# A two-branch attention kernel on one core: TensorE's order inside the recurrence written out by hand, and its weight loads moved from one DMA queue to another

## The chip, the core and the metric

The kernel runs on one core of a Trainium2 chip. The metric is device time in microseconds (us) of one execution. Engines are named as the profile names them: PE is TensorE (PEld its weight loads), DVE is VectorE, ACT is ScalarE, POOL is GpSimd and SP is SyncE; SPq, ACTq and POOLq are the queues through which these engines issue DMAs. "Granted clock" is the share of TensorE's full clock that it was given.

## What is computed

Two attention branches read the same x (2048 tokens of 576 features), and a sigmoid gate mixes their results row by row:

```python
x = A_x
g = _sigmoid((x * gate_w).sum(-1, keepdims=True))
a = _A_ref(x, A_mem0, A_Wq, A_Wk, A_Wv, A_Wo, A_seg_len)
b = _B_ref(x, B_wqkv, B_wo)
return g * a + (1 - g) * b
```

Branch A is a recurrence over 64 segments of 32 tokens. Each segment prepends 8 memory rows, projects the 40 rows to q, k and v with 32 heads of 128, applies masked softmax attention, projects back to 576 features with Wo, and hands its first 8 output rows on as the memory of the next segment:

```python
h = jnp.concatenate([mem, xs], axis=1)
...
o = jnp.einsum('bhte,hed->btd', o, Wo)
mem = o[:, :M, :].copy()
```

Branch B is plain softmax attention over all 2048 tokens with 32 heads of 18. It has no recurrence.

## The kernel before

**Stages.** A prologue (lines 318 to 467) transposes x, projects branch B's q, k and v into DRAM scratch (`qtd`, `ktd`, `vgd`), computes the gate and loads branch A's weights `wv`, `wq`, `wk` in 18 pieces, each one DMA (12 of 1 MB, 6 of 256 KB). `last_tokens` (line 287) then projects, for a batch of 16 segments, the last 8 tokens of each segment, which don't depend on the memory: 24 steps of 20 or 5 matmuls for the first batch before the recurrence, and 72 for the other three, which are fillers inside it. Then comes the recurrence (line 607), and at the end branch B's output projection with the gate (lines 750 to 812).

**Branch B as units.** Branch B's attention is a generator of 512 units, `b_steps`. A unit takes 512 queries and 128 keys of four heads: four score matmuls `sb` (line 208) into one PSUM tile of four banks, of which there is one buffer, two exponentials `etb` on ACT (line 229), and the four value matmuls `ob` (line 190) of the unit before. After 16 units the sums are turned and divided on DVE (lines 241 to 253, "the divide" below) and stored. `b_advance(1)` issues one unit; the kernel calls it between pieces of the prologue, inside the recurrence and in the end part.

**One segment of the recurrence.** `project` (line 631) multiplies the 32 rows `ht` with a quarter-packed weight block into PSUM (`pvv`), DVE copies it to `tm`; two such for each of q, k, v. `turn` transposes q and k (`pt`, line 647; DVE copies to `qt`, `kt`, line 652). The scores `psh` (line 677) go through an exponential on ACT (`et`, line 685) and a minimum on DVE that applies the mask (line 687). A matmul with a block of ones gives the sums `pss` (line 700), whose logarithm `lt` and the exponential of its negative `rq` (ACT, lines 702 and 704) give the reciprocal; DVE multiplies it in (line 705). The weighted values `pso` (line 713) are copied to `ot` (line 721), `out_project` multiplies with `wo` into `acc` (line 555) in two column spans, `split` takes each span apart into a high and a low half `hl` on DVE (lines 566 and 567), and `fold` (line 576) sums the packed quarters and transposes in one matmul (`pw3`); three copies put the first rows into the next `ht` (lines 738 to 740). Every fourth segment leaves a group of 32 last-token rows whose projection `finish_group` does one segment later. `fill` runs one step of `last_tokens`, or, when these are used up, four matmuls `idle` (line 485) whose result nobody reads. All these PSUM tiles share one tag `pb` with three buffers.

**What sets the order.** Nothing but a few manual edges is fixed by hand: a list scheduler orders each engine's instructions by its priorities and modelled readiness, within the data dependences. `tick()` spreads branch B's units over 16 places of a segment:

```python
per_tick = (total_steps - done[0] - NKB * 3 // 4) / n_seg / 16
```

The DMAs of one queue are issued in its order. The prologue's stores of projected q, k, v go through SP, and after every second store `store` places one piece of the weights behind it:

```python
d = nc.sync.dma_start(out=out, in_=in_)
stores[0] += 1
if stores[0] % 2 == 0:
    w = next(wgen, None)
```

POOL's queue carries the transposed x, the zero rows of `qtd` and `ktd` (`zt`) and the loads of branch B's `qch`, `kch` and `vch`.

Of the kernel before, what the change touches and what calls it, by code (L numbers as in the profile page):

```python
# [16 lines left out]
def kernel(  # L17
# [118 lines left out]
    def load_weights(w, src):  # L136
        w2 = src.rearrange("d h e -> d (h e)")
        for c in range(NF):
            yield nc.sync.dma_start(out=w[0][:, c, :], in_=w2[c * P:(c + 1) * P, :])
        for two in range(2):  # L140
            yield nc.sync.dma_start(
# [21 lines left out]
    def b_steps():  # L163
        kch, vch, qch = {}, {}, {}

# [15 lines left out]
        for gq in range(GB * NQC):  # L181
# [21 lines left out]
            for kb in range(NKB):  # L203
# [29 lines left out]
                before = ets  # L233
                yield
# [3 lines left out]
            HC = QC // 2  # L238
            for hf in range(2):
                tq = bint.tile([P, HC // 32, 32], FP32, name="tq")  # L240
                nc.vector.transpose(
                    out=tq[:, :, :].rearrange("p b e -> p (b e)"), in_=ob[:, hf * HC:(hf + 1) * HC]
                )
                rtb = bint.tile([P, HC // 32, 1], FP32, name="rtb")
# [10 lines left out]
                )  # L255
            if gq == GB * NQC - 1:
                last_stage.append(stage)
            else:
                for j in range(4):
                    f = (4 * g + j) * DhB  # L260
                    nc.sync.dma_start(
                        out=otd[f:f + DhB, qc * QC:(qc + 1) * QC], in_=stage[32 * j:32 * j + DhB, :]
                    )
# [58 lines left out]
    with ExitStack() as pctx:  # L322
# [16 lines left out]
        for n in range(NT):  # L339
# [22 lines left out]
            if (n + 1) * sn % SG == 0:  # L362
                q = (n + 1) * sn // SG - 1
                nc.gpsimd.dma_start(
# [3 lines left out]
        def all_weights():  # L368
            for w, src in ((wv, A_Wv), (wq, A_Wq), (wk, A_Wk)):
                yield from load_weights(w, src)  # L370

        wgen = all_weights()
        stores = [0]

        def store(out, in_):

            d = nc.sync.dma_start(out=out, in_=in_)
            stores[0] += 1
            if stores[0] % 2 == 0:
                w = next(wgen, None)  # L380
                if w is not None:
                    issue_behind(w, d)
# [10 lines left out]
        def project_qk(blk, share):  # L393
            stg = pw.tile([P, S], BF16, name="stg")
            for t in range(NQC):
# [10 lines left out]
                if share != 2 and t % 2 == 1:  # L406
                    b_advance(1)
            f = blk * P
            while f < (blk + 1) * P:
# [3 lines left out]
                store(out=(qtd, ktd)[which][h // 4, r:r + n, :], in_=stg[f - blk * P:f - blk * P + n, :])  # L413
# [10 lines left out]
        def project_vb(hf, ticks):  # L424
            for kb in range(NKB):
# [12 lines left out]
                store(  # L438
# [3 lines left out]
                if ticks != 2 and kb % 4 == 3:  # L442
                    b_advance(1)
# [26 lines left out]
    for i, _ in enumerate(last_tokens(0, 4)):  # L470
        b_advance(i % 2)
# [7 lines left out]
    def fill():  # L479
        if next(later, "end") == "end":  # L480
# [55 lines left out]
    pace = [0.0]  # L536
# [43 lines left out]

    pending = []

    def finish_group():

        if not pending:
            return
# [260 lines left out]
```

## Time and profile before

| what | value |
|---|---|
| median of 2 runs | 1947.96 us (1944.79 to 1951.13) |
| the profiled execution's own time | 1947.82 us |
| its span, first to last instruction | 1946.1 us |
| mean granted clock | 0.953 |
| busy, share of span | PE 88%, ACT 60%, DVE 49%, PEld 45%, POOL 9% |
| chain that ended last | PE 62%, ACT 16%, DVE 11%, DMA 6% |

A row of a group reads: line, engine, operation, output<-inputs, shapes, count, then total busy us and mean ns of one, then the idle time of the engine just before these instructions and who ended it. A row of the timeline reads: start, duration, engine, line, operation, count, and in brackets the idle time before it with its releaser. Matmuls are pipelined, so that a group of them is shorter than the sum of its durations, and a busy PE isn't PE at its peak.

### The profile page before, as it was taken

What the parts mean: (1) busy time and instruction counts of PE and PEld (TensorE: products, weight loads), DVE (VectorE), ACT (ScalarE), POOL (GpSimd) and SP (SyncE); (2) the same over time, 40 slices, a digit from 0 to 9 for tenths busy, and PEclk for the clock granted to TensorE, in tenths of its full rate; (3) what the DMA queues carried; (4) which work ended last, traced back from release to release, by engine and by line L of the source; (5) the groups of instructions that cost most, each with busy time, mean ns of one, the idle gap of its engine ahead of it and who ended that gap; (6) DMA issues with size and microseconds to landing.
All of it is one profiled execution on the core that took longest, in us unless ns stands there. A gap on an engine that the chain in (4) does not pass through costs nothing.

```text
span 1946.1 us, 58311 instructions
## 1 busy us (share of the span) xinstructions
PE 1704.6 (88%) x25310; PEld 876.9 (45%) x25310; DVE 945.1 (49%) x2113; ACT 1164.8 (60%) x1480; POOL 178.8 (9%) x411
## 2 busy tenths in 40 slices
PE   6388789999998999999999999999999998999977
PEld 3133354455544445455444544554444444444433
DVE  2022236555554555555555555554545554455445
ACT  2145433666665666666666666666666766666654
POOL 5100000100011000100001000100011000000000
PEclk9687899999998999999999999999999999999988
DMA  8932541221221111221111121211111110101023
GB/s 251 336 104 58 155 70 40 54 40 36 41 45 42 35 40 35 54 42 40 40 44 49 28 41 31 56 40 30 27 35 44 29 28 27 35 27 27 19 64 109
DMA packets 233451, 114.40 MB, mean 59 GB/s; under 512 B 166763, under 2 KB 223595, under 8 KB 231659
## 3 DMA queue, kind: packets, MB, share of 16 engines
q1 hardware_dynamic: 221348, 84.21, 17.2%
q0 software_dynamic: 6976, 20.19, 3.5%
q10 hardware_dynamic: 4871, 6.28, 1.0%
q8 instruction: 198, 3.24, 0.7%
q14 instruction: 58, 0.48, 0.1%
HBM read 57.72 MB, written 36.10 MB: 48 GB/s over the span
## 4 chain that ended last, share of the span: by engine, by line
PE 62%; ACT 16%; DVE 11%; DMA 6%; issue 3%; SPq 2%; ACTq 0%; DVEq 0%; POOL 0%; POOLq 0%
PE pvv L631 22%; ACT etb L229 12%; PE sb L208 9%; PE acc L555 7%; PE ob L190 6%; PE pt L647 3%; PE psh L677 3%; DVE ot L721 2%; PE pso L713 2%; PE pq L398 2%; ACT rq L704 2%; PE pv L294 2%; ACT lt L702 2%; DVE hl L566 1%; DVE hl L567 1%
## 5 line engine op out<-in xcount | busy, mean ns | idle before, releaser
L229 ACT ACTIVATE etb<-sb 128x1024 bf16<-128x1024 f32 x1024 | 993.2, 1020 | 581.4 <-PE sb L208 556.0
L640 DVE CAST tm<-pvv 128x512 bf16<-128x512 f32 x384 | 264.6, 689 | 244.5 <-PE pvv L631 244.3
L190 PE MATMUL ob<-etb,vch 128*32 128x512 bf16 x2048 | 318.6, 399 | 41.4 <-ACT etb L229 28.8
L208 PE MATMUL sb<-qch,kch 32*128 32x512 bf16 x2048 | 269.6, 395 | 50.5 <-ACT etb L229 34.4
L631 PEld LDWEIGHTS <-ht 128*32 128x32 bf16 x7680 | 202.9, 97 | 187.7 <-issue 24.1
L555 PE MATMUL acc<-wo,ot 128*32 128x384 bf16 (+1 forms) x4096 | 211.9, 296 | 28.4 <-DVE ot L721 23.9
L208 PEld LDWEIGHTS <-kch 32*128 32x128 bf16 x2048 | 76.7, 91 | 207.5 <-issue 170.0
L190 PEld LDWEIGHTS <-vch 128*32 128x32 bf16 x2048 | 83.8, 93 | 179.0 <-issue 153.0
L555 PEld LDWEIGHTS <-ot 128*32 128x32 bf16 x4096 | 115.8, 98 | 98.2 <-DVE ot L721 63.6
L631 PE MATMUL pvv<-wv_m,ht 128*32 128x512 bf16 x2048 | 152.6, 384 | 0.0
L631 PE MATMUL pvv<-wq_m,ht 128*32 128x512 bf16 x2048 | 139.8, 386 | 11.7 <-DVE ht L738 11.4
L721 DVE CAST ot<-pso 128x320 bf16<-128x320 f32 x256 | 113.7, 484 | 50.8 <-PE pso L713 50.5
L631 PE MATMUL pvv<-wk_m,ht 128*32 128x512 bf16 x2048 | 137.2, 379 | 0.2 <-ACT vl L283 0.2
L705 DVE TENSOR_TENSOR et<-et,rq 128x320 bf16<-128x320 bf16 x128 | 41.1, 321 | 159.6 <-ACT rq L704 152.6
L566 DVE CAST hl<-acc 128x384 bf16<-128x384 f32 (+1 forms) x160 | 72.7, 454 | 84.6 <-PE acc L555 83.1
L285 DVE CAST vl<-pv 128x512 bf16<-128x512 f32 x90 | 61.7, 687 | 76.2 <-PE pv L306 20.6
L685 ACT ACTIVATE et<-psh 128x320 bf16<-128x320 f32 x128 | 52.9, 445 | 69.9 <-PE psh L677 69.9
L713 PE MATMUL pso<-et,v_sb 64*128 64x40 bf16 x2048 | 62.7, 177 | 36.0 <-DVE et L705 30.5
L713 PEld LDWEIGHTS <-v_sb 64*128 64x128 bf16 x2048 | 56.1, 93 | 67.2 <-issue 59.7
L623 POOL COPY qt<-xl 128x256 bf16<-128x256 bf16 x64 | 26.4, 412 | 618.8 <-issue 576.3
L647 PE MATMUL pt<-ident,tm 128*128 128x128 bf16 x1024 | 75.8, 220 | 2.0 <-DVE tm L640 2.0
L702 ACT ACTIVATE lt<-pss 128x320 f32<-128x320 f32 x128 | 56.3, 440 | 32.9 <-PE pss L700 32.4
(118 smaller groups left out, 1815.4 us busy)
## 6 DMA issues: line engine op xcount, KB each, us to landing
v_sb<-tm SPq DMA_DIRECT2D x512, 32.0 KB
wo<-in_A_Wo_dram SPq DMA_DIRECT2D x4, 1152.0 KB
wv_m<-in_A_Wv_dram SPq DMA_DIRECT2D x4, 1024.0 KB
qch<-qtd POOLq DMA_DIRECT2D x32, 128.0 KB, 2.5
wq_m<-in_A_Wq_dram SPq DMA_DIRECT2D x4, 1024.0 KB
kch<-ktd POOLq DMA_DIRECT2D x32, 128.0 KB, 2.8
vgd<-vt SPq DMA_DIRECT2D x32, 128.0 KB
wk_m<-in_A_Wk_dram SPq DMA_DIRECT2D x4, 1024.0 KB
```

Source lines behind the costliest of these rows:

```text
L190: mm = nc.tensor.matmul(ob[32 * j:32 * j + 32, :], lhsT=vc[:, o + 32 * j:o + 32 * j + 32], rhs=ets[j // 2][:, j % 2, :], start=(kb == 0), ...
L208: mm = nc.tensor.matmul(sb[:, j, :], lhsT=kc[32 * j:32 * j + 32, o:o + P], rhs=qch[gq][32 * j:32 * j + 32, :], start=True, stop=True, tile ...
L229: nc.scalar.activation(out=etb[:, :, :], in_=sb[:, 2 * jp:2 * jp + 2, :], func=ACT.Exp, scale=scale_b)
L285: nc.vector.tensor_copy(out=out, in_=in_)
L555: nc.tensor.matmul(acc[32 * j:32 * j + 32, 0:d1 - d0], lhsT=o[:, h, t0:t0 + CT], rhs=wo[:, h, d0:d1], start=(b == 0 and i == 0), stop=(b = ...
L566: nc.vector.tensor_copy(out=hl[:, 0, d0:d1], in_=acc[:, 0:d1 - d0])
L631: nc.tensor.matmul(pv[32 * j:32 * j + 32, :], lhsT=ht[:, cc, :], rhs=rw, start=(c == 0), stop=(c == NF), tile_position=(0, 32 * j),)
L640: nc.vector.tensor_copy(out=tm[:, :], in_=pv[:, :])
L647: nc.tensor.transpose(out=pt[:, i, :, :].rearrange("p j t -> p (j t)"), in_=tm2[i // 4][:, (i % 4) * Dh:(i % 4 + 1) * Dh], identity=ident[ ...
L702: nc.scalar.activation(out=lt[:, :], in_=pss[:, 0:W8], func=ACT.Ln)
L713: nc.tensor.matmul(pso[:, i * L:(i + 1) * L], lhsT=v_sb[64 * jj:64 * jj + 64, b * 1024 + i * Dh:b * 1024 + (i + 1) * Dh], rhs=et[64 * jj:6 ...
L721: nc.vector.tensor_copy(out=ot[:, j * HG:(j + 1) * HG, :].rearrange("p h t -> p (h t)"), in_=pso[:, 0:W8])
```

## The change

**Weights.** The 18 pieces of `wv`, `wq`, `wk` move from SP's queue to POOL's. The first waits for the last store of `xld`, and each next one for the landing of the one before. SP keeps only the stores.

**Units.** In the prologue `b_advance(1)` is called after each of the four steps of a q/k block (before: every second), after every second step of the v blocks (before: every fourth) and after every step of `last_tokens` (before: every second): 56 calls where there were 28. In the recurrence a segment issues exactly seven units through `slot()`, where it issued 7.4 on average by `tick()`.

**Order.** The recurrence stands under `manual_schedule` for PE alone: PE executes its instructions in the order in which the program writes them. The other engines are still ordered by the scheduler; the exponentials and logarithms of the recurrence get a higher priority (`AHEAD`). The text of a segment is rewritten: both scores, then a fill (or the group's projection), then both sums, a unit, both weighted values, the output projection with a unit inside, a unit, three of five folds, a second fill (or the group's rows), and the other two folds. The second fill runs only real steps, no idle matmuls.

**Smaller edits.** The divide is cut: the two transposes stay at the end of the 16 units, and the rest of each half is issued during one of the next units (`late`), its store included. In the end part the scaling with `omg` is on ACT for all rows (before: on DVE for three quarters of them).

The diff, cut to its core:

```diff
-            yield nc.sync.dma_start(out=w[0][:, c, :], in_=w2[c * P:(c + 1) * P, :])
+            yield nc.gpsimd.dma_start(out=w[0][:, c, :], in_=w2[c * P:(c + 1) * P, :])
...
                 before = ets
+                if late and kb > 0:
+                    f, *args = late.pop(0)
+                    f(*args)
                 yield
...
+        before = xlast
+        for w, src in ((wv, A_Wv), (wq, A_Wq), (wk, A_Wk)):
+            for d in load_weights(w, src):
+                tc.add_manual_dep(
+                    d.ins,
+                    before.ins.name,
+                    mybir.DependencyInfo(mybir.DependencyClass.Sync, mybir.DependencyReason.DATA),
+                    reason="one piece at a time",
+                )
+                before = d
...
-                if share != 2 and t % 2 == 1:
+                if share != 2:
                     b_advance(1)
...
-                if ticks != 2 and kb % 4 == 3:
+                if ticks != 2 and kb % 2 == 1:
                     b_advance(1)
...
-    for i, _ in enumerate(last_tokens(0, 4)):
-        b_advance(i % 2)
+    for _ in last_tokens(0, 4):
+        b_advance(1)
...
+    ordered.enter_context(tc.manual_schedule(engines={mybir.EngineType.PE}))
...
+        tq2 = [project(wq, starts[0])]
+        slot()
+        tq2.append(project(wq, starts[1]))
+        tk2 = [project(wk, starts[0])]
+        slot()
+        tk2.append(project(wk, starts[1]))
+        turn(tq2, qt)
+        project_v(0)
+        slot()
+        turn(tk2, kt3)
+        project_v(1)
+        scores(0)
+        slot()
+        scores(1)
+        group = bool(pending)
+        if group:
+            group_project()
+        else:
+            fill()
+        normalize(0)
+        normalize(1)
+        slot()
+        weigh(0)
+        weigh(1)
+        hl = seg2.tile([P, 2, Dm], BF16, name="hl")
+        acc = ps_a.tile([P, 512], FP32, name="acc", tag="pb")
+        out_project(acc, ot, 0, 0, *WSPAN[0])
+        slot()
+        out_project(acc, ot, 0, 1, *WSPAN[0])
+        split(acc, hl, *WSPAN[0])
+        acc = ps_a.tile([P, 512], FP32, name="acc", tag="pb")
         for b in range(2):
-            out_project(acc1, ot, 0, b, *WSPAN[1])
-            tick()
-        split(acc1, hl, *WSPAN[1])
-        pw3 = fold(hl)
+            out_project(acc, ot, 0, b, *WSPAN[1])
+        split(acc, hl, *WSPAN[1])
+        slot()
+        pw3 = fold_tile()
+        fold(hl, pw3, range(3))
+        if group:
+            group_rows()
+        else:
+            fill(False)
+        fold(hl, pw3, range(3, NF + 1))
```

How it moves instructions, at three places. First, SP's queue in the prologue before the change, where `stg` holds a projected block and `wv_m` is the weight of v:

```order
L377 DMA qtd_85<-stg_380 18x2048 x2
L139 DMA wv_m_96<-in_A_Wv_dram 128x4096
L377 DMA qtd_85<-stg_380 18x2048 x2
L139 DMA wv_m_96<-in_A_Wv_dram 128x4096
L377 DMA qtd_85<-stg_380 18x2048 x2
L139 DMA wv_m_96<-in_A_Wv_dram 128x4096
L377 DMA qtd_85<-stg_380 18x2048
L377 DMA qtd_85<-stg_380 2x2048
L139 DMA wv_m_96<-in_A_Wv_dram 128x4096
L377 DMA qtd_85<-stg_421 10x2048
```

And POOL's queue at the same stage with the change (`kch`, `vch`, `qch` are branch B's loads):

```order
L139 DMA wv_m_96<-in_A_Wv_dram 128x4096
L169 DMA kch_740<-ktd_86 128x512
L169 DMA kch_744<-ktd_86 128x512
L177 DMA qch_748<-qtd_85 128x512
L177 DMA qch_1120<-qtd_85 128x512
L139 DMA wv_m_96<-in_A_Wv_dram 128x4096
L171 DMA vch_734<-vgd_87 128x512
L169 DMA kch_1579<-ktd_86 128x512
L169 DMA kch_1610<-ktd_86 128x512
L139 DMA wv_m_96<-in_A_Wv_dram 128x4096
L171 DMA vch_738<-vgd_87 128x512
```

SP's stores stand alone now, and it is branch B's loads that stand between the pieces of the weights, each of which waits for the one before it.

Second, ACT in one segment that has fills, before:

```order
L685 ACTIVATE et_1955<-psh_14005 128x320
L229 ACTIVATE etb_14033<-sb_14024 128x1024
L229 ACTIVATE etb_14035<-sb_14024 128x1024
L685 ACTIVATE et_1955<-psh_14037 128x320
L229 ACTIVATE etb_14088<-sb_14079 128x1024
L229 ACTIVATE etb_14090<-sb_14079 128x1024
L702 ACTIVATE lt_14123<-pss_14121 128x320
L704 ACTIVATE rq_14125<-lt_14123 128x320
L229 ACTIVATE etb_14181<-sb_14172 128x1024
L229 ACTIVATE etb_14183<-sb_14172 128x1024
L702 ACTIVATE lt_14204<-pss_14202 128x320
L704 ACTIVATE rq_14206<-lt_14204 128x320
```

and in one with the change:

```order
L693 ACTIVATE et_2375<-psh_13199 128x320
L230 ACTIVATE etb_13227<-sb_13218 128x1024
L693 ACTIVATE et_2375<-psh_13231 128x320
L230 ACTIVATE etb_13229<-sb_13218 128x1024
L706 ACTIVATE lt_13276<-pss_13274 128x320
L707 ACTIVATE rq_13277<-lt_13276 128x320
L706 ACTIVATE lt_13283<-pss_13281 128x320
L230 ACTIVATE etb_13297<-sb_13288 128x1024
L707 ACTIVATE rq_13284<-lt_13283 128x320
L230 ACTIVATE etb_13299<-sb_13288 128x1024
```

The second logarithm `lt` now follows the first pair directly, where two `etb` lay between; one `etb` stands between it and its `rq`.

Third, DVE at the end of a segment with a fill, with the change (`vl` is the copy of the second fill's result, `ht0` the memory rows for the next segment):

```order
L573 CAST hl_12316<-acc_12317 128x384
L574 TENSOR_TENSOR hl_12316<-acc_12317,hl_12316 128x384
L573 CAST hl_12316<-acc_12374 128x192
L574 TENSOR_TENSOR hl_12316<-acc_12374,hl_12316 128x192
L300 CAST vl_12435<-pv_12429 128x512
L772 CAST ht0_2369<-pw3_12422 128x4x8
L773 CAST ht0_2369<-pw3_12422 64x8
```

Before the change no `vl` stood between the split and the memory rows, since the fill's matmuls were done earlier in the segment.

More of the change, by code (lines that the diff above doesn't have):

```diff
@@ L255, in b_steps @@
                 )
+                if hf == 1 and gq < GB * NQC - 1:
+                    for j in range(4):
+                        f = (4 * g + j) * DhB
+                        nc.sync.dma_start(
+                            out=otd[f:f + DhB, qc * QC:(qc + 1) * QC], in_=stage[32 * j:32 * j + DhB, :]
+                        )
+            for hf in range(2):
+                late.append((divide, hf, tqs[hf], stage, gq))
             if gq == GB * NQC - 1:
+                while late:
+                    f, *args = late.pop(0)
+                    f(*args)
                 last_stage.append(stage)
[L258 to L263, printed above, removed]
     bgen = b_steps()
```

113 lines of the change are left out of this document (43 added, 70 removed).

## The prediction

> **What bounds the kernel now.** I read the windows first, to see the stages, then the timeline of each. The windows of the prologue (span's stretch and length, then busy us and count of PE, PEld, DVE, ACT, POOL, granted clock, DMA share, GB/s):
>
> ```profile
> 26.10:62.30 36.20, 14.47 (x75) 6.46 (x75) 4.42 (x10) 4.00 (x10) 10.50 (x21) 0.74 0.90 279
> 62.30:82.00 19.70, 6.92 (x30) 3.71 (x29) 1.11 (x3) 0.99 (x2) 2.12 (x4) 0.67 0.93 326
> 130.00:200.00 70.00, 57.18 (x294) 21.53 (x293) 15.22 (x30) 36.90 (x43) 0.54 (x1) 0.76 0.23 57
> ```
>
> and the same view for the exponentials and their matmuls alone, by stage (two `etb` are one unit of branch B):
>
> ```profile
> 82.00:268.90 186.90, 37.74 (x166) 82.52 (x84) 0.79 0.46 119
> 268.90:1855.30 1586.40, 265.61 (x1800) 871.83 (x900) 0.99 0.16 38
> 1879.80:1946.10 66.30, 10.89 (x52) 24.96 (x26) 0.79 0.40 120
> ```
>
> So there are three limits. Until 82 us no unit has run, PE stands still for most of the time and the DMA engines are 90% busy. From there to 268.9 us, where the first segment starts, 42 units run. The recurrence takes 1586 us for 63 segments and 450 units; the last segment and the end part take the rest, with 13 units after 1879.8. Why PE waits early, from the timeline and the view of waits:
>
> ```profile
> L139 SPq DMA_DIRECT2D wv_m<-in_A_Wv_dram x4: 417/2183/2604, 36.6 to 55.1; - x4
> ...
> 61.65 0.59 ACT L283 CAST stg<-pq 128x512 bf16<-128x512 f32 x1 [20.87 <-DMA qtd<-stg]
> 62.28 2.29 PE L398 MATMUL pq<-xT,wb 128*128 128x512 bf16 x5 [21.73 <-ACT stg L283]
> 82.03 0.61 PE L208 MATMUL sb<-qch,kch 32*128 32x512 bf16 x4 [12.81 <-DMA kch<-ktd]
> 165.66 0.62 PE L208 MATMUL sb<-qch,kch 32*128 32x512 bf16 x4 [0.30 <-ACT etb L229]
> 168.38 0.62 PE L208 MATMUL sb<-qch,kch 32*128 32x512 bf16 x4 [0.30 <-ACT etb L229]
> ...
> DVE vt L285 <- DMA vgd<-vt: 56.3, 10, 20.2
> ```
>
> The third projected block can't leave PSUM until a `stg` buffer is stored, and the stores stand on SP among four 1 MB pieces: 21.7 us of PE, then 12.8 for the keys, which need that block. The first unit starts at 82.0. From then on a lone unit takes 168.38 - 165.66 = 2.72 us, bound by its two exponentials, since `sb` has one buffer.
>
> In the recurrence I take one segment of seven units without a divide as the standard:
>
> ```profile
> L738 DVE CAST ht<-pw x63: 152/191/192, 293.8 to 1854.8; 128x32 bf16<-128x32 f32 x63
> ...
> 899.57 1.05 PE L631 MATMUL pvv<-wq_m,ht 128*32 128x512 bf16 x16 [0.28 <-DVE ht L738]
> 908.02 0.39 PE L208 MATMUL sb<-qch,kch 32*128 32x512 bf16 x4
> 908.53 1.94 ACT L229 ACTIVATE etb<-sb 128x1024 bf16<-128x1024 f32 x2
> 908.68 0.58 PE L677 MATMUL psh<-qt,kt 128*64 128x40 bf16 x16
> 912.31 0.30 PE L700 MATMUL pss<-et,bsel 128*128 128x320 bf16 x1
> 913.65 0.38 PE L208 MATMUL sb<-qch,kch 32*128 32x512 bf16 x1
> 914.07 0.68 DVE L285 CAST vl<-pv 128x512 bf16<-128x512 f32 x1
> 916.58 0.31 PE L700 MATMUL pss<-et,bsel 128*128 128x320 bf16 x1
> 916.99 0.44 ACT L702 ACTIVATE lt<-pss 128x320 f32<-128x320 f32 x1
> 917.46 0.47 ACT L704 ACTIVATE rq<-lt 128x320 bf16<-128x320 f32 x1
> 917.96 0.32 DVE L705 TENSOR_TENSOR et<-et,rq 128x320 bf16<-128x320 bf16 x1 [2.41 <-ACT rq L704]
> 918.34 0.48 PE L713 MATMUL pso<-et,v_sb 64*128 64x40 bf16 x16 [0.47 <-DVE et L705]
> 919.27 1.47 PE L555 MATMUL acc<-wo,ot 128*32 128x384 bf16 x32 [0.46 <-DVE ot L721]
> 920.54 0.56 DVE L566 CAST hl<-acc 128x384 bf16<-128x384 f32 x1 [0.93 <-PE acc L555]
> 921.78 0.36 DVE L566 CAST hl<-acc 128x192 bf16<-128x192 f32 x1
> 922.87 0.19 DVE L738 CAST ht<-pw 128x32 bf16<-128x32 f32 x1 [0.34 <-PE pw L576]
> 923.43 1.05 PE L631 MATMUL pvv<-wq_m,ht 128*32 128x512 bf16 x16
> ```
>
> The mean segment is (1854.8 - 293.8) / 62 = 25.18 us; this one took 23.86. Up to 913.65 PE is packed: 14.08 us. The other 9.8 us are a ladder PE-ACT-DVE-PE, run twice, with holes.
>
> **The change part by part. Prologue.** The stores lose their 1 MB neighbours. Without the weights' issue and transfer ahead of them I put the third block's copy near 43 us instead of 61.65, and the first unit, behind the keys, at 58 (estimate; 52 if the keys land at once, 75 if the traffic of the zero rows and of the piece in flight holds them). The v blocks then pace the first five units: 16 stores through two buffers `vt`, some 3.5 us a pair once the queue is free, until about 80 (the waits row shows 56 us lost there before). A program order that puts 52 units ahead of the first projection of a segment and five between it and the next makes the rest a matter of units: PE and ACT can't do one faster than 2.72 us, and with blocks between I take 2.85 for 25 of them, 2.75 for 22 and 2.5 for the last five: 80 + 7 (30 matmuls in one piece) + 71 + 3 + 60 + 13 = 234 for the second projection, against 270 before. **Term: -36** (from -15, if the first unit moves little, to -50). The weights have slack: piece by piece at 7 to 12 us they land by 130 to 210, `wk` being needed near 200; branch B's loads stand behind pieces 2 to 7, which costs at most one landing each while units are few.
>
> **Recurrence.** In a segment with fills the packed part keeps its work but for one fill half behind the sums: 14.08 - 1.12 - 0.13 = 12.8 us from the first projection to the end of the fill. Then the ladder, now once for both halves, by the rows' durations with the gaps seen there (0.03 on ACT, 0.06 to 0.10 between engines); a unit costs PE 908.68 - 908.02 = 0.66. Zero is the end of the second score's exponential; the fill ends at 0.77. Sums until 1.3, the unit until 1.65. ACT still has one `etb` of the unit before (to 0.97), so `lt` runs 1.27 to 1.71, `rq` to 2.2, the product to 2.56: first values 2.62. The second `lt` ends at 2.67, but then ACT's order has an `etb` (0.97): second `rq` to 4.13, product to 4.48, second values 4.54 to 4.95. PE has nothing else in that time: holes of 1.0 and 1.5 us. Output projection and units: 0.7, 0.66, 0.7, 0.86, 0.66, to 8.7. Three folds to 9.2, the fill to 10.4, two folds to 10.7; `vl` (0.68) is ahead of the memory rows on DVE, so these start at 11.2 and the next projection at 11.43. From there 10.04 to the end of the first scores, and ACT's exponential, `etb`, exponential make 2.0: the segment closes at **23.46**, 0.4 under the standard one.
>
> Segments with a group do 64 narrow matmuls
>
> ```profile
> 883.58 2.34 PE L555 MATMUL acc<-wo,otl 128*32 128x384 bf16 x62
> L485 PE MATMUL idle<-wv_m,ident 128*128 128x512 bf16 x164 | 43.7, 385 | 0.0
> ```
>
> in place of the first fill, 1.2 us more, of which 0.3 was waiting anyway, and ten folds, a copy and five transposes for the second: 24.3. After the 72 real fills are used up (36 segments of 48), twelve have one idle fill (43.7 / 41 = 1.07 us) early, which waiting covers, and none late, with no `vl`: 21.6. Sum for 63: 36 x 23.46 + 15 x 24.3 + 12 x 21.6 = 1468.
>
> To this come two costs in the form of accidents. A divide (two turns of 0.43, two each of reciprocal, product and turn back)
>
> ```profile
> L253 DVE STREAM_TRANSPOSE stage<-tn 128x256 bf16<-128x256 bf16 x64 | 28.2, 440 | 1.2
> L241 DVE STREAM_TRANSPOSE tq<-ob 128x256 f32<-128x256 f32 x64 | 27.3, 427 | 48.5 <-PE ob L190 48.4
> L247 DVE TENSOR_TENSOR tn<-tq,rtb 128x256 bf16<-128x256 f32 x64 | 27.0, 422 | 1.7
> ```
>
> puts up to 2.5 us of DVE before a minimum or a split in about half of 28 cases: 0.4 a segment (0 to 0.8). And the clock:
>
> ```profile
> 938.07:941.48 3.41, 3.24 (x48) 1.38 (x47) 1.49 (x5) 2.46 (x4) 0.54 (x1) 1.00 0.36 97
> 941.48:944.89 3.41, 2.10 (x39) 1.01 (x37) 3.31 (x11) 2.21 (x3) 0.53 (x1) 1.00 0.90 142
> 944.89:948.30 3.41, 3.41 (x53) 1.92 (x45) 1.53 (x4) 1.94 (x2) 0.00 (x0) 0.50 0.13 36
> ```
>
> A stretch of 3.41 us with PE busy for only 2.10 of it, drains counted in, is followed by one at half clock. The new holes give every segment such a stretch if the windows fall right, a third to a half of the time, and a dip costs about 1.4 us of the output projection: 0.5 a segment (0 to 1.4). The Trainium skill ("TensorE: Matmul & The Clock Gate", Part 1) says that the clock halves after an idle window of about 3.4 us; by that a hole of 1.5 us costs nothing, and the sum would lose this term; the trace speaks against it, since a window 60% busy was enough.
>
> 1468 + 63 x 0.9 = 1525 against 1586. **Term: -62** (-125 if the ladder is 1 us shorter, +15 if it is 1.2 longer).
>
> **End.** Eight units after the last segment for 13: -15 at 2.9; ACT takes over 24 scalings of some 0.5 us between them, and more output rows come after the last unit: +10. **Term: -5** (-12 to +6).
>
> **Sum.** The profiled span of 1946.1 minus 36, 62 and 5 is 1843; with the 1.7 us that the execution's 1947.8 lies above its span, **1845**. The median of the runs, 1948.0, is the same as that execution's time.
>
> **The rivals.** (1) *No clock dips*: 63 x 0.5 = 32 less, **1813**. For it: segments in which the holes fall across two windows. Against it: the rows at 944.89. The Trainium skill's rule of the clock gate, named above, would give this rival. (2) *The queue doesn't matter, only the issuing*: then the weights keep the DMA engines as full as before (279 to 326 GB/s) and only the four issues of at most 2.2 us median are saved, 9 of 36: **1872**. For it: 90% DMA share. Against it: the stores, not the engines' totals, are what PE waited for. The Trainium skill ("Trainium Kernel Development and Optimization", Key Constraints) says that DMAs of all queues run on the same 16 engines and that issuing from several saves only issue time, which is this rival. (3) *The fixed order's holes are wider*: each of the two waits costs 0.4 more, since PE may not pull anything forward as it did at 912.31 to 913.65, where it worked between `lt` and the product; 63 x 0.8 = 50: **1895**. For it: a ladder of eight hops in which I counted no queue but the ordered ones. (4) *Slower:* the 21 PSUM tiles of a segment go through three buffers, and PE, fixed, can't go round a copy that is late. It waits for DVE now. At 0.15 us for each tile this is 21 x 0.15 x 63 = 198: **2043**; it decides from 0.08 a tile, where it eats the 103 gained. Against it:
>
> ```profile
> DVE tm L640 <- PE pvv L631: 244.3, 350, 2.0
> ```
>
> in 350 of 384 cases DVE stood ready for the projection's result. That the order isn't what the change says is excluded by the rows of PE's order: seven units stand at the same places in every segment.
>
> **How the numbers follow.** Forecast 0.44, no dips 0.16, queue without effect 0.14, wider holes 0.22, late copies 0.04. A measurement can tell about 2% from no change, 39 us, so faster means under 1909: all of the first three and, with what scatters around 1895, 0.09 of the 0.22, together 0.83; the other 0.13 are the same; 0.04 slower. The range from 1785 (prologue and recurrence both near their better ends) to 1915 (wider holes with a small gain in the prologue) leaves out some 2 in 10.
>
> **What would show it.** Right: no wait of PE for `stg` of 20 us; the first unit between 52 and 75 us; the first segment near 225; segments of 23 to 24.5 us, the late ones without group near 22; holes of about 1 and 1.5 us before the values, the second ended by DVE behind `rq`, `rq` behind an `etb`; stretches at half clock in a quarter to a half of the segments. Wrong: a first unit at 80, a segment of 25, PE waiting for PSUM copies, values waiting for the DMA of `v_sb`, or an end part that grows by 20.

## The result, and the profile after

| | before | after |
|---|---|---|
| median | 1947.96 us (1944.79 to 1951.13) | 1840.53 us (1840.00 to 1841.05) |
| after / before | | 0.9448, 95% interval 0.9381 to 0.9516 |
| profiled span | 1946.1 us | 1838.3 us |
| mean granted clock | 0.953 | 0.925 |

The time is 4.5 us from the forecast of 1845. The three terms of which that was made are not: two were too small and one was nearly absent. First the stages after, as windows cut where the forecast cut them: the third q/k block's last projection, the first unit, the end of the first v blocks, the second projection of the first segment, the last `ht` copy. Columns as before.

```profile
0.00:58.34 58.34, 31.70 (x232) 17.70 (x232) 14.66 (x37) 12.68 (x39) 30.24 (x60) 0.88 0.85 242
58.34:67.21 8.87, 6.06 (x30) 3.43 (x29) 0.84 (x2) 0.98 (x2) 3.60 (x7) 0.80 0.54 156
67.21:99.48 32.27, 19.78 (x96) 8.38 (x97) 3.21 (x7) 11.46 (x16) 4.99 (x11) 0.74 0.65 191
99.48:267.81 168.33, 138.88 (x999) 58.41 (x1001) 39.44 (x79) 107.27 (x121) 14.27 (x26) 0.88 0.58 152
267.81:1759.46 1491.65, 1311.36 (x23205) 677.00 (x23197) 843.80 (x1889) 995.10 (x1259) 132.69 (x326) 0.94 0.16 39
1759.46:1838.30 78.84, 60.56 (x643) 31.28 (x643) 33.23 (x78) 46.65 (x70) 0.40 (x1) 0.82 0.36 106
```

The same view for `etb` alone (PE, ACT, clock, DMA share, GB/s; two `etb` are a unit):

```profile
67.21:99.48 32.27, 3.81 (x18) 9.83 (x10) 0.74 0.65 191
99.48:267.81 168.33, 44.41 (x206) 99.73 (x104) 0.88 0.58 152
```

So 57 units stand ahead of that second projection, as the order said (42 before), but it comes at 267.8 us and not at 234: before, it came at 270.0. The recurrence from there to the last `ht` copy took 1491.7 us (before 1584.8), and the end 78.8 (before 91.3). Those are -2, -93 and -12.5, against the forecast's -36, -62 and -5. The prologue's timeline, all engines, shows its first stall still there:

```profile
57.70 0.58 ACT L298 CAST stg<-pq 128x512 bf16<-128x512 f32 x1 [16.14 <-DMA qtd<-stg]
58.34 2.29 PE L409 MATMUL pq<-xT,wb 128*128 128x512 bf16 x5 [16.99 <-ACT stg L298]
...
67.21 0.39 PE L209 MATMUL sb<-qch,kch 32*128 32x512 bf16 x1 [2.81 <-DMA kch<-ktd]
```

Without 1 MB pieces ahead of the stores PE waits 17.0 us where it waited 21.7. Next, one segment without group or divide, in the timeline:

```profile
411.50 1.05 PE L645 MATMUL pvv<-wq_m,ht 128*32 128x512 bf16 x16 [0.79 <-DVE ht L772]
...
423.34 0.43 ACT L693 ACTIVATE et<-psh 128x320 bf16<-128x320 f32 x1
...
424.20 0.43 PE L702 MATMUL pss<-et,bsel 128*128 128x320 bf16 x2
...
425.88 1.02 ACT L230 ACTIVATE etb<-sb 128x1024 bf16<-128x1024 f32 x1
425.93 0.47 PE L715 MATMUL pso<-et,v_sb 64*128 64x40 bf16 x16 [0.47 <-DVE et L708]
...
426.79 0.47 ACT L707 ACTIVATE rq<-lt 128x320 bf16<-128x320 f32 x1
...
427.67 0.48 PE L715 MATMUL pso<-et,v_sb 64*128 64x40 bf16 x16 [1.26 <-DVE et L708]
...
434.26 1.05 PE L645 MATMUL pvv<-wq_m,ht 128*32 128x512 bf16 x16 [0.79 <-DVE ht L772]
```

It took 22.76 us. The second `rq` stands behind an `etb`, the hole it leaves is 1.26 us, and the segment closes 10.49 us after the second exponential ends at 423.77 (forecast 11.43). This is one of the segments at full clock. Most had a stretch at half clock; in windows (the clock is the first number behind POOL's count):

```profile
881.14:884.55 3.42, 1.69 (x48) 1.16 (x48) 1.99 (x6) 3.13 (x6) 0.00 (x0) 1.00 0.26 73
884.55:887.97 3.42, 3.42 (x52) 1.40 (x44) 0.65 (x3) 1.92 (x2) 0.40 (x1) 0.50 0.39 62
887.97:891.38 3.41, 2.77 (x70) 2.05 (x58) 2.34 (x6) 1.96 (x3) 0.00 (x0) 1.00 0.00 0
```

The two holes leave PE busy for 1.69 us of a window, and the whole next window, which holds the output projection, is at half clock. Between the first and the last `ht` copy I counted 48 such windows after and 12 before.

### The profile page after: what moved, and what is told of

It is laid out like the page before. It is cut to its first block, busy times and chain, and to the rows that moved or that the text cites. A ratio compares the mean times of both kernels' runs of the same rounds, so it can differ in the third digit from the quotient of the medians.

```text
span 1838.3 us, 58046 instructions
## 1 busy us (share of the span) xinstructions
PE 1568.3 (85%) x25198; PEld 796.2 (43%) x25198; DVE 935.2 (51%) x2089; ACT 1174.1 (64%) x1504; POOL 186.2 (10%) x429
## 4 chain that ended last, share of the span: by engine, by line
PE 63%; DVE 12%; ACT 11%; DMA 7%; issue 4%; SPq 3%; DVEq 0%; ACTq 0%
PE pvv L645 23%; PE acc L562 9%; PE sb L209 8%; ACT etb L230 7%; PE ob L191 7%; PE pt L660 3%; PE pso L715 3%; DVE ot L723 3%; PE pq L409 2%; PE psh L684 2%; DVE et L708 2%; DMA vgd<-vt 2%; ACT et L693 2%; DVE vl L300 2%; SPq L674 1%
## 5 line engine op out<-in xcount | busy, mean ns | idle before, releaser
L645 PEld LDWEIGHTS <-ht 128*32 128x32 bf16 x7680 | 188.6, 97 | 222.2 <-DVE ht L772 50.2
L191 PE MATMUL ob<-etb,vch 128*32 128x512 bf16 x2048 | 245.6, 417 | 19.6 <-ACT etb L230 18.8
L209 PE MATMUL sb<-qch,kch 32*128 32x512 bf16 x2048 | 220.3, 411 | 30.3 <-ACT etb L230 23.7
L562 PE MATMUL acc<-wo,ot 128*32 128x384 bf16 (+1 forms) x4096 | 197.8, 347 | 0.0
L645 PE MATMUL pvv<-wq_m,ht 128*32 128x512 bf16 x2048 | 139.5, 393 | 44.1 <-DVE ht L772 43.8
L209 PEld LDWEIGHTS <-kch 32*128 32x128 bf16 x2048 | 61.5, 92 | 201.2 <-issue 187.4
L645 PE MATMUL pvv<-wv_m,ht 128*32 128x512 bf16 x2048 | 134.0, 382 | 0.0
L191 PEld LDWEIGHTS <-vch 128*32 128x32 bf16 x2048 | 60.0, 94 | 162.6 <-issue 156.5
L544 POOL COPY ht<-xg 128x144 bf16<-128x144 bf16 x64 | 19.6, 307 | 711.6 <-PE pvv L645 649.8
L695 DVE TENSOR_TENSOR et<-et,cap 128x320 bf16<-128x320 bf16 x128 | 45.2, 353 | 73.6 <-ACT et L693 73.6
L684 PEld LDWEIGHTS <-kt 128*64 128x64 bf16 x2048 | 61.5, 112 | 43.5 <-DVE kt L665 28.9
```

The lines of the kernel that those rows point to most:

```text
L191: mm = nc.tensor.matmul(ob[32 * j:32 * j + 32, :], lhsT=vc[:, o + 32 * j:o + 32 * j + 32], rhs=ets[j // 2][:, j % 2, :], start=(kb == 0), ...
L209: mm = nc.tensor.matmul(sb[:, j, :], lhsT=kc[32 * j:32 * j + 32, o:o + P], rhs=qch[gq][32 * j:32 * j + 32, :], start=True, stop=True, tile ...
L562: nc.tensor.matmul(acc[32 * j:32 * j + 32, 0:d1 - d0], lhsT=o[:, h, t0:t0 + CT], rhs=wo[:, h, d0:d1], start=(b == 0 and i == 0), stop=(b = ...
L645: nc.tensor.matmul(pv[32 * j:32 * j + 32, :], lhsT=ht[:, cc, :], rhs=rw, start=(c == 0), stop=(c == NF), tile_position=(0, 32 * j),)
L684: nc.tensor.matmul(psh[64 * jj:64 * jj + 64, i * L:(i + 1) * L], lhsT=kt[:, h * L:h * L + 64], rhs=qt[:, h, :], start=True, stop=True, til ...
```

## The experiments

One table for all. "First unit" and "second stage" (the first `wk` projection, just behind the second projection) are starts; the recurrence runs from the first to the last `ht` copy; "half" counts the 3.41 us windows at half clock in it. Ratios are to the kernel before on the same chip.

| kernel | median us | ratio, 95% interval | first unit | second stage | recurrence | half | end |
|---|---|---|---|---|---|---|---|
| before | 1947.96 | | 82.0 | 271.4 | 1561.0 | 12 | 91.3 |
| after | 1840.53 | 0.9448 (0.9381 to 0.9516) | 67.2 | 269.9 | 1468.7 | 48 | 78.8 |
| a_sp | 1863.20 | 0.9544 (0.9502 to 0.9587) | 80.8 | 283.1 | 1479.9 | 57 | 78.4 |
| b_pool | 1938.45 | 0.9941 (0.9920 to 0.9961) | 66.4 | 258.0 | 1559.2 | 8 | 91.2 |
| a_sched | 1803.84 | 0.9254 (0.9218 to 0.9291) | 68.9 | 262.8 | 1430.0 | 30 | 77.4 |
| a_small | 1852.79 | 0.9503 (0.9462 to 0.9544) | 67.9 | 271.2 | 1487.2 | 59 | 80.4 |
| a_idle | 1789.38 | 0.9175 (0.9140 to 0.9210) | 66.9 | 267.4 | 1423.9 | 6 | 77.0 |
| a_rq | 1816.48 | 0.9310 (0.9273 to 0.9347) | 66.8 | 267.6 | 1446.7 | 48 | 78.9 |
| a_dve | 1843.40 | 0.9452 (0.9401 to 0.9503) | 67.8 | 272.3 | 1471.3 | 52 | 79.1 |
| a_calls | 1904.32 | 0.9767 (0.9723 to 0.9810) | 67.3 | 254.0 | 1465.4 | 48 | 160.2 |
| s_idle | 1764.32 | 0.9043 (0.9017 to 0.9068) | 67.8 | 255.5 | 1396.4 | 0 | 78.2 |
| s_idle_c8 | 1773.50 | 0.9096 (0.9070 to 0.9122) | 66.4 | 262.6 | 1411.6 | 0 | 70.8 |
| s_idle_rq_zt | 1746.23 | 0.8955 (0.8933 to 0.8977) | 66.2 | 258.6 | 1385.1 | 1 | 77.4 |
| a_idle_mv | 1786.63 | 0.9152 (0.9128 to 0.9176) | 65.9 | 269.6 | 1417.1 | 9 | 80.9 |

The stage columns are those of one profiled execution each. That execution took 5.9 us less than the median of its kernel in b_pool and s_idle, 6.5 less in a_sched and 8.7 more in a_small; in the others it is within 3.6.

### The weights' queue: a_sp and b_pool

a_sp is the changed kernel with the old placing of the weights; b_pool the kernel before with the new one alone.

```diff
-            yield nc.gpsimd.dma_start(out=w[0][:, c, :], in_=w2[c * P:(c + 1) * P, :])
+            yield nc.sync.dma_start(out=w[0][:, c, :], in_=w2[c * P:(c + 1) * P, :])
...
+            if stores[0] % 2 == 0:
+                w = next(wgen, None)
```

> The changed kernel with one part undone: the weights stand on SP's queue again, one piece behind every second store; order, units and the small edits stay. Theory (the queue matters: the move took the first unit from 82.0 to 67.2 us, and the later stores of the prologue have lost their 1 MB neighbours too): the third stg copy goes from 57.7 back to near 61.7, the first unit to about 82, the second projection of the first segment from 267.8 to 280 to 290, the time to 1853 to 1863. Rival (the 16 DMA engines were the limit, not the queue; and what is gained at 67 us is lost again before 268, since the units wait for other stores): the first unit moves by less than 5 us, the second projection by less than 5, time 1838 to 1846.

> The kernel before with one part of the change alone: the weights on POOL's queue, one piece at a time. Theory (the queue matters): first unit from 82.0 to about 68, first segment from 268.9 to about 255, time 1933 to 1938. Rival (DMA engines are the limit): first unit and first segment within 5 us of before, time 1943 to 1950. A third way: without the calls of the changed kernel PE has no units to pull forward, and the early gain ends at another wait; then the first unit is early and the first segment is not.

Rows of the instructions that read or write `ht`, first in a_sp, then in b_pool (the two numbers after the durations are the first and the last start):

```profile
L650 PE MATMUL pvv<-wk_m,ht x2048: 379/379/634, 283.1 to 1790.5; 128*32 128x512 bf16 x187
```

```profile
L626 PE MATMUL pvv<-wk_m,ht x2048: 379/379/390, 258.0 to 1845.5; 128*32 128x512 bf16 x187
```

The move is worth 13.2 us at the first segment in the one kernel (283.1 to 269.9) and 13.4 in the other (271.4 to 258.0), and it is already there at the first unit (13.6 and 15.6). That is a_sp's theory; its time stands just above the range. The move does matter, then, at little more than half of the 24 us that I gave it at the first unit. b_pool is at 0.9941 of before, some 11 us; its interval leaves out 1, but it is less than the 2% that the prediction took for the least change to be told. What the move saved shows in SP's own rows, two of them before and two after:

```profile
42.93 2.60 SPq L139 DMA_DIRECT2D wv_m<-in_A_Wv_dram  x1
45.58 4.36 SPq L377 DMA_DIRECT2D qtd<-stg  x2
```

```profile
34.04 19.71 SPq L424 DMA_DIRECT2D qtd<-stg  x12
53.79 10.27 SPq L424 DMA_DIRECT2D ktd<-stg  x12
```

From the first store to the end of the 24th, the last of the first `ktd` block, SP took 44.1 us before. The issues of 11 weight pieces among them held it for 10.4 of these (0.36 to 2.60 each), the issues of the stores for 20.5. After, the same 24 stores took 30.0 us, with 22.8 for their issues. So most of the 14.0 us is issuing, as rival 2 had it; the rest is less waiting between the stores. The edit also puts the pieces off, each behind the landing of the one before (five had been issued by 58 us before, one after), and whether another queue alone would do as much wasn't tried.

In a_sp the recurrence, which the edit doesn't touch, is 11.2 us longer with 9 half-clock windows more: about 1.2 us each.

### PE's fixed order: a_sched

```diff
-    ordered.enter_context(tc.manual_schedule(engines={mybir.EngineType.PE}))
```

> The changed kernel with TensorE left to the scheduler again: the text, the seven units, the two fills and the raised priority of the exponentials and logarithms stay. Theory (the fixed order of TensorE itself brings the recurrence's 93 us): mean segment from 23.7 back to about 25, time 1915 to 1935. Rival (the text's order, seven units in every segment and the priorities bring it, and the scheduler keeps to them): mean segment 23.5 to 24.2, time 1830 to 1870.

Both were wrong: with the scheduler the changed text is 37 us *faster*, and the intervals don't meet. Groups by line, after and then a_sched:

```profile
L645 PE MATMUL pvv<-wq_m,ht 128*32 128x512 bf16 x2048 | 139.5, 393 | 44.1 <-DVE ht L772 43.8 <-DVE ht L532 0.4
L715 PE MATMUL pso<-et,v_sb 64*128 64x40 bf16 x2048 | 64.2, 179 | 106.2 <-DVE et L708 99.7 <-DMA v_sb<-tm 5.6
```

```profile
L644 PE MATMUL pvv<-wq_m,ht 128*32 128x512 bf16 x2048 | 145.1, 381 | 8.3 <-DVE ht L771 5.5 <-DVE ht L532 0.6
L714 PE MATMUL pso<-et,v_sb 64*128 64x40 bf16 x2048 | 63.4, 178 | 42.1 <-DVE et L707 35.0 <-DMA v_sb<-tm 4.3
```

The scheduler keeps the seven units near their places but cuts them up. PE's timeline in one segment of a_sched:

```profile
421.55 0.39 PE L191 MATMUL ob<-etb,vch 128*32 128x512 bf16 x2 [0.55 <-ACT etb L230]
422.27 0.55 PE L714 MATMUL pso<-et,v_sb 64*128 64x40 bf16 x16 [0.32 <-DVE et L707]
...
428.99 0.39 PE L191 MATMUL ob<-etb,vch 128*32 128x512 bf16 x1
429.36 0.40 PE L209 MATMUL sb<-qch,kch 32*128 32x512 bf16 x4
429.85 1.05 PE L644 MATMUL pvv<-wq_m,ht 128*32 128x512 bf16 x16
```

One or two `ob` matmuls, or an `sb`, go between the two weighted values and ahead of the next projection, where the fixed order waits 44 us in all for the memory rows. So the gain of the recurrence belongs to the rest of the change, not to the fixed order, which gives 39 us of it back. That rest is the rewritten text, the priorities, the cut divide (next run) and fewer units: 434 in these 62 segments where there were 448, some 9 us by the prediction's 0.66 us of PE for one (an estimate). The text and the priorities weren't tried apart.

### The small edits: a_small

```diff
-            if gq == GB * NQC - 1:
-                while late:
+            while late:
...
+                    nc.vector.tensor_scalar_mul(out=btmp[:, :], in0=po[:, 0:Dm // 2], scalar1=omg[:, n:n + 1])
```

> The changed kernel with the two small edits undone: the divide is whole again at the end of 16 units, and in the end part DVE scales three quarters of the output rows. They act in different stages, so one kernel shows both. Theory: the cut divide is worth 0.4 us a segment (the whole one holds DVE for some 2.7 us ahead of a split or a minimum in half of its 28 places), so the recurrence is 15 to 30 us longer, and the end part from the last ht copy to the end goes from 78.8 to 72 to 88. Rival (the divide's DVE work lies where DVE waits for TensorE anyway): recurrence within 6 us of 1468.7. Time by the theory 1850 to 1875, by the rival 1835 to 1850.

In the profiled execution the whole divide makes the recurrence 18.5 us longer, inside the theory's range, and eleven half-clock windows more, at 1.2 us each 13 of the 18.5, come with it. But that execution is 8.7 us above the median of its kernel, and the medians are only 12.3 apart, so that the divide is worth 10 to 18 us. The end is 1.6 us longer: moving the scaling to ACT cost nothing that shows.

### The clock: a_idle

```diff
                 pso = ps_a.tile([P, 512], FP32, name="pso", tag="pb")
+                if j == 1:
+                    for c in range(NF):
+                        nc.tensor.matmul(
+                            pso[:, :], lhsT=ident[:, :], rhs=wv[0][:, c, 0:512], start=(c == 0), stop=(c == NF - 1)
+                        )
```

> The changed kernel with four matmuls more in each segment, 128x512, whose result nobody reads: they stand ahead of the second weighted values, in the hole of 1.26 us. Nothing else is changed, and no work is left out. Theory (a window of 3.41 us in which TensorE is busy for less than 2.2 is followed by one at half clock, and each such one costs a segment 1.2 us): the 48 half-clock windows of the recurrence fall under 10, the recurrence from 1469 to 1420 to 1430, time 1790 to 1802, though TensorE has more to do. Rival (a hole of 1.3 us is no idle window; the half clock has another cause): as many half-clock windows as before, time 1838 to 1850.

The theory held, but for the time, which came out 0.6 us below its range: 256 matmuls more, 51 us less.

```profile
L716 PE MATMUL pso<-wv_m,ident 128*128 128x512 bf16 x256 | 66.3, 382 | 0.0
L720 PE MATMUL pso<-et,v_sb 64*128 64x40 bf16 x2048 | 63.0, 177 | 45.1 <-DVE et L708 39.9 <-DMA v_sb<-tm 3.9
```

The wait ahead of the values shrank from 106 to 45 us because the idle matmuls stand in it. The order of everything else on PE and ACT is the same, on DVE but for four products of the divide, and 42 half-clock windows went. (1468.7 - 1423.9) / 42 = 1.07 us each, net of what the idle matmuls cost.

### ScalarE's order: a_rq

```diff
+                    if last_rq[0] is not None:
+                        issue_behind(ex, last_rq[0])
```

> The changed kernel with one thing of ScalarE's order fixed: in a segment the exponentials of branch B wait behind the second rq, so that lt, rq, lt, rq stand together. Theory (the exponential between the second lt and the second rq costs the second values 0.75 us a segment, as the hole of 1.26 us ended by rq shows): second hole 0.5 us, 47 us less in the recurrence; and the smaller hole leaves TensorE busier, so that half-clock windows fall from 48 to under 15, worth 40 more: time 1750 to 1800. Rival (what is put back is sb, which has one buffer: TensorE waits for the late exponential at the next unit, in the output projection): time 1830 to 1850.

Neither: 24 us faster, where the theory had at least 40. The timeline of a segment:

```profile
873.01 0.44 ACT L710 ACTIVATE lt<-pss 128x320 f32<-128x320 f32 x1
...
873.48 0.47 ACT L711 ACTIVATE rq<-lt 128x320 bf16<-128x320 f32 x1
873.85 0.49 DVE L727 CAST ot<-pso 128x320 bf16<-128x320 f32 x1 [0.51 <-PE pso L719]
...
874.25 0.32 DVE L712 TENSOR_TENSOR et<-et,rq 128x320 bf16<-128x320 bf16 x1
...
874.62 0.59 PE L719 MATMUL pso<-et,v_sb 64*128 64x40 bf16 x16 [0.76 <-DVE et L712]
```

`rq` is ready 0.3 us before the product, which now waits behind an `ot` copy on DVE; the hole is 0.76 instead of 1.26. That the half-clock windows stay at 48 speaks against the theory's second half: 41 of the full-clock windows still have PE busy for less than 2.21 us, where after the change 51 had.

### The prologue: a_dve and a_calls

```diff
-    for _ in last_tokens(0, 4):
+    for _ in last_tokens(0, 0):
```

> The changed kernel with all copies of the prologue's second part (stg, vt, vl, from the point where units run) on DVE; before, every fourth is on ScalarE. Theory (in ScalarE's queue a copy that waits for a store's landing holds up the exponentials behind it, some 25 us in all between 98 and 258 us): the second projection of the first segment from 267.8 to 245 to 257, time 1818 to 1830. Rival (the stores themselves pace the copies, on whichever engine they are, and TensorE waits for them in order): second projection within 5 us of 267.8, time 1835 to 1846.

The rival held (270.1 against 267.8, time unchanged): on whichever engine the copies are, the stores pace them. The copies to `vt` waited 56.6 us for stores of `vgd`, where they waited 61.1 after the change. For a_calls the edit is that of the calls, with two units more ahead of each of the end part's loads so that the divides still come first:

```diff
-    for _ in last_tokens(0, 4):
-        b_advance(1)
+    for i, _ in enumerate(last_tokens(0, 4)):
+        b_advance(i % 2)
```

> The changed kernel with the calls for units in the prologue as before (28 instead of 56), so that about 15 units less are done by the first segment and 15 more in the end part. Theory (a unit costs its 2.5 to 2.7 us of ScalarE in the prologue as in the end part; the prologue lost its forecast gain to the 15 units more that it does): the second projection from 267.8 to 225 to 240, the end from 78.8 to 110 to 120, time 1834 to 1848. Rival A (the prologue's waits for stores have room for units, which cost little there): second projection 250 to 262, end 110 to 120, time 1860 to 1875. Rival B (a unit is dearer in the prologue, because of what stands in ScalarE's queue): second projection below 220, time 1815 to 1830.

Windows of `etb` in a_calls, of the prologue and from the end of the last segment on (the last `ht` copy is at 1739.2):

```profile
67.30:254.00 186.70, 27.18 (x112) 56.50 (x58) 0.76 0.62 164
...
1761.00:1899.40 138.40, 40.54 (x152) 71.92 (x74) 0.64 0.20 59
```

29 units in the prologue where the change has 57, and 37 in the end where it has 9: under the fixed order nothing is pulled forward, so 28 moved, not 15. They save 16 us there (0.57 each) and cost 81 in the end part (2.9 each). That is rival A's mechanism at twice its count.

### Towards a better kernel: s_idle, s_idle_c8, s_idle_rq_zt, a_idle_mv

s_idle joins the edits of a_sched and a_idle. s_idle_c8 adds `b_advance(2 if i < 8 else 1)` in the steps of `last_tokens`; s_idle_rq_zt adds the edit of a_rq and puts the zero rows' DMAs ahead of the loop that transposes x.

> TensorE left to the scheduler (as in the run that took the fixed order away) and the four idle matmuls ahead of the second weighted values. Theory (the scheduler gains 0.63 us a segment by putting branch B's values and scores into the holes, above all between the folds and the next projection, and the idle matmuls take most of its 30 half-clock windows away, at 1.2 us each): recurrence from 1430 to 1395 to 1410, half-clock windows under 10, time 1765 to 1783. Rival (both fill the same hole, so that the gains don't add): recurrence 1420 to 1430, time 1789 to 1804.

> The same with eight units more in the prologue, behind the first eight steps of the last tokens' projection, so that eight less are left for the end part. Theory (the run with fewer calls paid 2.9 us for each unit in the end part and saved 0.6 in the prologue, so each unit moved the other way gains some 2): second projection of the first segment 5 to 20 us later, end part 15 to 25 us shorter, time 5 to 15 below that of the kernel without the eight. Rival (there TensorE and ScalarE are already bound by units of 2.72, and the end part waits for its DMAs, not for units): second projection 20 us later, end part less than 10 shorter, time 10 to 20 above.

> The same as the first, and two things more that act in different stages: the exponentials wait behind the second rq in a segment, and the 3.5 MB of zero rows are issued ahead of the transposed x on POOL's queue, not behind it. Recurrence, theory (the rq's place cost the fixed order 0.35 us a segment): 15 to 25 us below the first kernel; rival (the scheduler has moved other work there): within 6 us. Prologue, theory (from 35 to 55 us the DMA engines are full with the zero rows, and the stg stores and the third copy at 57.7 wait for these, not for the queue): third pq projection from 58.3 to 44 to 50 and the first unit from 67.2 to 52 to 60; rival (the x loads then come late by as much): both within 4 us of before, or later.

The gains of s_idle add, to 72 us of the recurrence where the two alone make 84: 1396.4, no half-clock window left. The eight further units were a loss, 9 us: 7 us were saved in the end, 7 spent in the prologue, and the recurrence came out 15 longer. Its first two segments (`etb` alone, in s_idle and then in s_idle_c8) say why:

```profile
282.08:327.58 45.50, 8.11 (x56) 27.90 (x29) 1.00 0.17 48
288.73:347.23 58.50, 16.69 (x84) 40.78 (x42) 1.00 0.14 38
```

Of the eight units the scheduler put six or seven into these two segments, which took 13.0 us more; about one stood ahead of them. So they weren't moved into the prologue, and what they would cost there remains open. The order of `rq` was worth 11.3 us of the recurrence, between theory and rival. The zero rows, in PE's timeline:

```profile
51.37 1.24 PE L413 MATMUL pq<-xT,wb 128*128 128x512 bf16 x5 [1.38 <-ACT stg L302]
52.45 3.23 PE L445 MATMUL pvb<-wb,xT 128*128 128x288 bf16 x25
64.87 1.36 PE L445 MATMUL pvb<-wb,xT 128*128 128x288 bf16 x5 [9.20 <-DVE vt L304]
66.16 0.60 PE L210 MATMUL sb<-qch,kch 32*128 32x512 bf16 x1
```

The third block's stall is gone (1.38 us for 17). But PE comes to it later, so that its projection starts only 7.0 us earlier than after the change, at 51.4, not between 44 and 50. The first unit hardly moves, where the theory had 52 to 60. It stands on PE behind a v projection that now waits 9.2 us for a `vt` buffer. This kernel is the fastest that was run, 0.8955 of before.

a_idle_mv asks what the scheduler does that the hand didn't:

```diff
-        slot()
+        if s == 0:
+            slot()
...
         if s + 1 < n_seg:
+            slot()
```

> TensorE's order fixed, the four idle matmuls as in the earlier run, and one unit of each segment moved: the one behind the first projection stands behind the last fold instead, where TensorE waits 0.7 us for the memory rows in every segment (42.6 us in all). Theory (the 28 us between the fixed order's 1423.9 and the scheduler's 1396.4, both with the idle matmuls, are this one place, which the fixed order leaves empty): recurrence 1395 to 1405, time 1760 to 1772. Rival (the unit's sb isn't free there, because its two exponentials of the unit before run until then, so that TensorE waits for ScalarE in place of the rows, and only the scheduler's cutting of units into single matmuls helps): recurrence 1415 to 1430, time 1780 to 1795.

The recurrence got 6.8 us shorter, which is in the rival's range; the time fell by 2.8, within what the runs scatter. PE's timeline at the moved unit:

```profile
880.58 0.26 PE L582 MATMUL pw<-sel,hl 128*128 128x32 bf16 x4
881.13 0.40 PE L209 MATMUL sb<-qch,kch 32*128 32x512 bf16 x4 [0.30 <-ACT etb L230]
881.46 0.40 PE L191 MATMUL ob<-etb,vch 128*32 128x512 bf16 x4
```

It waits for `sb`. In segments with a second fill between the two units the median still fell from 22.76 to 22.45 us; in the late ones without a fill it rose from 21.46 to 22.30. So one place doesn't settle the 28 us between a_idle and s_idle; that the cutting of units is the rest was not tried by itself.

## Why the prediction was right, and where it was not

The time was right by luck, because errors cancelled: 34 us too much in the prologue, 31 too little in the recurrence, 7.5 too little in the end.

**Prologue (-36, measured -2).** The step that failed is "makes the rest a matter of units". The first segment came at 256.3, not near 225. The first unit came at 67.2, not 58; the v blocks paced units until 99.5, not 80 (5 units in 32.3 us); the other 52 took 168.3 us, 3.24 each, not 2.5 to 2.85. PE is busy for 139 of these 168 us at a clock of 0.88: its own projections and the waits for stores fill the time, so units were cheap there (0.57 us by a_calls). By this the term is: queue -13, 15 more units 15 x 0.57 = +8.5, sum -4.5. The forecast's sum of 234 also has a 3 for which it names no row. That the units had to pay 2.75 was a price of a lone unit, taken from 165.66 to 168.38 in the kernel before, where PE and ACT ran nothing else.

**"The third block's copy near 43 us"** was wrong: 57.70. I took the 1 MB pieces for the cause of the stall; they were 4 us of it. Early zero rows took 7 us off, and the first unit stood at 66 all the same. Rival 2 gave the queue 9 us and the forecast gave it 24 at the first unit; 13 to 16 were measured, most of it by rival 2's mechanism, the issuing (its 9 counted four of the 11 pieces). The Trainium skill ("Trainium Kernel Development and Optimization", Key Constraints) says that a second issuing engine saves issue time only; the trace agrees in the main, with 10.4 us of weight issues out of the 14.0 that SP saved.

**Recurrence (-62, measured -93).** The ladder's steps stand in the order that was written, but its sum was too long: 22.76 for 23.46, and between the starts of the `ht` copies, at full clock, 23.4 for 24.3 with a group and 21.15 for 21.6 late. Counted from 423.77, the second values came at 3.90 and not at 4.54, 0.44 of it since the sums had ended at 0.86 (424.20 + 0.43) and not at 1.3; the stretch behind the values was 0.3 shorter, the packed part 0.23 longer (12.27). The accidents, 0.9 forecast, came to 1.1: the mean segment is 1468.7 / 62 = 23.69, and 35, 15 and 12 segments at the three values give 22.6. Of this the clock is 48 x 1.07 / 62 = 0.8, where 0.5 was forecast: the holes tripped it in 46 of the 62 segments, not in a third to a half. The rest is 0.2, where the forecast had 0.4 for the divides; no run shows what it consists of.

**Where the gain comes from** I had only half: the term was worked out for the ladder, run once for both halves, and that is right; but nothing in it came from PE being fixed, and rival 3's mechanism (PE may not pull anything forward) is real at 39 us. It was hidden in the total, since the rest gained more.

**Clock (rival 1).** Wrong, as a_idle shows. The Trainium skill's rule ("TensorE: Matmul & The Clock Gate", Part 1: the clock falls after an idle window of about 3.4 us) doesn't cover it: PE was busy for 41 to 65% of the windows that were followed by half clock, but for one (0.74 us).

**End (-5, measured -12.5).** The 15 us for five units fewer were right in size (2.9 each by a_calls); the +10 for scaling on ACT wasn't there (a_small).

**Rival 4** (late PSUM copies) left no trace: in the view of waits no row has PE behind a `tm` copy.

## What to carry to other kernels

A forecast of a total is no test of its terms: cut the result at the forecast's own stage bounds. Before an order is fixed by hand, build the same text with the scheduler: here the fixed order was a loss of 37 us inside a gain of 107. Where TensorE has holes of a microsecond in every period, count the windows at half clock: here four idle matmuls in the hole of each segment gained 51 us.

## What the runs showed of the hardware

The half clock follows how long PE was busy in the window before. All stretches at half clock in the recurrence after start on one grid of 3.413 us, to within 1 ns, and no window of that grid had a mixed clock. Of its full-clock windows, 331 had PE busy for 2.21 us or more, and one of them (2.22) was followed by half clock; of 51 with less 46 were. Each cost about 1.1 us (a_idle).

The bound isn't that sharp in every trace. In a_sched 19 of the 30 half-clock windows followed one with 2.22 to 2.40 us. In all 14 traces, 220 of 231 full-clock windows with PE busy for less than 2.0 us were followed by half clock, and none of 5072 with 2.42 or more.

The grid runs free of the segments, whose lengths are no multiple of it. The time of an execution goes with its clock: the four of a_sched took 1797.4, 1801.3, 1806.4 and 1806.7 us at mean clocks of 0.943, 0.938, 0.933 and 0.935. That the same program meets the grid at another place each time would explain it; no trace shows that.
